# Masks by recurrences on VectorE and a new order of the first stretch in a chain of attention, feed-forward and routed experts

## The chip, the cores and the metric

The kernel runs on one core of a Trainium2 chip. The metric is the device time of one execution in microseconds. Instructions of each engine (TensorE, VectorE, ScalarE, GpSimd) run in the order in which they were issued to that engine; loads and stores are issued by the sequencers of SyncE (SP) or ScalarE and move on 16 DMA engines. The profile calls TensorE's matmuls PE and its weight loads PEld, VectorE DVE, ScalarE ACT and GpSimd POOL.

## The reference

Three layers stand one behind the other, on 1536 tokens of width 512 (2 batches, 8 heads of 64, sequence 768).

1. Linear attention with decay. Each head has a decay `lam`. Per block of 64 positions the output is `(q k^T * Dmask) v + (q * lam^(pos+1)) state`, with `Dmask[i, j] = lam^(i-j)` for `i >= j` and 0 elsewhere, and then `state = lam^64 * state + (k * lam^(63-pos))^T v`.
2. A dense feed-forward: `h = x w_in` (2048 wide), `g = elu(h)`, `x = g w_out`. The two weight matrices come in as 64-bit floats.
3. A routed layer: `logits = x w_gate` (8 experts), a skip score `x w_skip`; a token whose score is positive goes to its best expert, `x + gate * relu(x w1[e]) w2[e]`; the others pass through.

Everything is wanted at float32 accuracy.

## The kernel before, in words

The attention is rewritten over chunks of 128 tokens, 12 in all, 6 to a batch. Three chunks make a block of 384 tokens, and there are four blocks. For a chunk `c` the plan knows these steps, which also name what is issued: `S` scores on PE (16 matmuls, L251), `M` the multiplication of the scores by the decay mask on DVE (two halves, L261), `KD` and `QD` the products of k and q with powers of the decay on POOL (L284, L278), `KV` k times v on PE (L454), `ST` and `DEC` the update of the state (ST on DVE, L481, for chunk 0 on ACT; DEC on ACT, L461), `V` and `I` the two products that make the output on PE (L293), and `XH` and `XL` the split of the output into a high part (ACT, L437) and a remainder (DVE, L441), which together are the activations `xT` of the feed-forward.

The feed-forward works with pairs of high part and remainder too, and three matmuls stand for one product. A weight piece `f` (16 of them, 1 MB each as 64-bit words) is turned into such a pair by `CV` (ACT, L162), three bit operations `B0`, `B1`, `B2` (DVE, L174, L177, L180), `HI` (ACT, L185) and `LO` (DVE, L191). One step `n` of the feed-forward is `F1` (12 matmuls of 384 columns, L506), the activation `R`, `X` (ACT, L511, L514), `E` (DVE, L526), `GH` (ACT, L532), `GL` (DVE, L537), and `F2` (9 matmuls of 512 columns, L553). There are 64 steps, 16 for each of four blocks; the first 32 take the first two blocks in a mixed order, so that a weight piece is wanted only about every second step.

The string `PLAN` (L38) lists the order in which the steps of the first batch's attention and of feed-forward steps 0 to 22 are issued; each engine sees its own steps in that order. The rest is issued by loops. Late in the kernel the last block is routed: transposes (L593), logits (L608: 128 weight columns against 9 moving columns, for four parts, two instructions each), a pick of the expert on DVE (L666 to L676), one-hot tiles (L699), and matmuls that gather the rows of expert 0 (L1055, L1024); then eight experts follow, each with matmuls L1112 and L1137.

Before the plan begins the tables of the decay are made. `lam` is loaded to 8 partitions of `z8`; seven multiplications (L774) double a row of powers up to `lam^128`; the row is written to DRAM (`z_dr`, L777) and read back by one DMA as `mask`, 128 partitions of 8 overlapping windows (L788). Two kinds of matmuls spread the powers: a transpose for `kd` (L823) and four matmuls for `lp` (L825), which hold the factors of KD and QD. Groups of matmuls on zeros (`warm`, L817) stand ahead and behind: 6 and 5 of them, two instructions each.

The loads: `lam` goes out on SP, `f0`, `v0` and `q0` on ACT's queue. The next SP issues are ordered one after another by hand: the write of `z_dr`, q1, v1, the read of `mask`, and then q2, v2, q3, v3, f1, q4, v4, f2, q5, v5, f3, f4 and the rest (here `q` is the pair of q and k for the scores, `v` the pair of k and v by rows, 0.5 MB each).

Of the kernel before, what the change touches and what calls it, by code (L numbers as in the profile page):

```python
# [61 lines left out]
def kernel(  # L62
# [203 lines left out]

    qd_t = {}

    def at_qd(c):
        if c % CPS:  # L270
            if c == 1:
                qd = mid.tile([P, 2, TB], F32, tag="g", name="g", bufs=3)
                qd = qd.rearrange("p s t -> p (s t)")[:, 0:4 * P].rearrange("p (k i) -> p k i", k=4)
            elif c < CPS:
                qd = ph[0].tile([P, 4, P], F32, tag="qd", name="qd", bufs=1)
            else:
                qd = t2()
# [471 lines left out]


    if True:
        alloc_chunk(0)
        alloc_chunk(1)
        alloc_chunk(2)
        z8 = ph[0].tile([H, ZW], F32, tag="v", name="z8", bufs=2)
        sel = t2()[0:H]
        nc.sync.dma_start(out=z8[:, P + 1:P + 2], in_=lam.rearrange("(h o) -> h o", o=1))
        load_ff(0, nc.scalar)
        dma_kv(0, nc.scalar)
        dma_kq(0, nc.scalar)  # L760
        nc.vector.memset(z8[:, 0:P], 0.0)
        nc.vector.memset(z8[:, P:P + 1], 1.0)
# [15 lines left out]
        zt = z_dr[:, :]
        toep = bass.AP(tensor=zt.tensor, offset=zt.offset + 1, ap=[[1, P], [ZW, H], [1, P]])
        for c in range(CPB, CPS):  # L780
            alloc_chunk(c)
        lead = zw.ins
        with tc.issue_after(lead):
            lead = dma_kq(1).ins
        with tc.issue_after(lead):
            lead = dma_kv(1).ins
        with tc.issue_after(lead):
            mr = nc.sync.dma_start(out=mask, in_=toep)  # L788
# [34 lines left out]
        nc.tensor.transpose(out=kdb[:, 0:H], in_=z8[:, P:2 * P], identity=ident[0:H, 0:H])  # L823
        for k in range(4):
            nc.tensor.matmul(out=lpb[:, k * P:(k + 1) * P], lhsT=sel[:, k, :],  # L825
                             rhs=z8[:, P + 1:2 * P + 1], start=True, stop=True)
        warm(idle_bank, WARM[1])
        nc.vector.tensor_copy(out=kd, in_=kdb[:, 0:H].rearrange("p (h o) -> p h o", o=1))
        nc.scalar.activation(out=lp, in_=lpb.rearrange("p (k i) -> p k i", k=4), func=ACTF.Copy)
# [502 lines left out]
```

## Time and profile before

| | us |
|---|---|
| median of three executions | 442.74 (440.9 to 442.75) |
| the profiled execution: its time | 444.0 |
| its span in the trace | 441.8 |

| engine | busy in the span |
|---|---|
| PE | 426.9 us, 97% |
| PEld | 374.1 us, 85% |
| DVE | 326.3 us, 74% |
| ACT | 239.5 us, 54% |
| POOL | 74.1 us, 17% |

Times in the profile count from the start of the span; the 2.2 us by which the execution is longer lie around it. The ends of matmuls are modelled, so a busy PE may still be held up: the count of matmuls in a stretch tells more than its busy time. [...] DVE's busy share is an average over very unlike stretches: it is nearly full from 25 to 100 us, where weight pieces are converted, and about 60% from 100 to 200 us.

### The profile page before, as it was taken

How to read it: one execution, taken by the hardware profiler on the slowest of the kernel's cores; microseconds unless marked ns; L12 is line 12 of the kernel's file. 1: busy time of each engine (PE TensorE's matmuls, PEld its weight loads, DVE VectorE, ACT ScalarE, POOL GpSimd, SP SyncE). 2: the span in 40 equal slices, each digit the busy share in tenths (PEclk: the TensorE clock that was granted, in tenths of full speed). 3: DMA queues.
4: the chain of work that ended last, by engine and by line, in shares of the span. 5: the costliest groups of instructions: out<-in, count | busy, mean ns of one | idle time of the engine just before them, and what ended most of it. 6: DMA issues, size and time to landing. Idle time of an engine off the chain costs nothing.

```text
span 441.8 us, 8027 instructions
## 1 busy us (share of the span) xinstructions
PE 426.9 (97%) x3087; PEld 374.1 (85%) x3087; DVE 326.3 (74%) x701; ACT 239.5 (54%) x401; POOL 74.1 (17%) x104
## 2 busy tenths in 40 slices
...
GB/s 310 394 420 415 274 47 82 244 121 191 32 2 72 6 116 99 144 24 191 56 134 62 73 190 191 119 118 174 162 208 194 304 326 372 376 370 384 159 2 35
DMA packets 28704, 79.45 MB, mean 180 GB/s; under 512 B 4306, under 2 KB 9434, under 8 KB 26608
## 3 DMA queue, kind: packets, MB, share of 16 engines
...
## 4 chain that ended last, share of the span: by engine, by line
PE 68%; DVE 15%; DMA 6%; issue 5%; ACT 3%; SPq 2%; POOL 1%; POOLq 0%; ACTq 0%; DVEq 0%
PE h L506 23%; PE y L553 18%; PE h L1112 8%; PE y L1137 6%; PE aux L553 5%; DVE v L177 3%; DMA big<-in_wff_dram 2%; DMA xe<-blank 2%; DVE v L180 2%; DVE wa L191 2%; DVE g L537 1%; ACT v L162 1%; PE aux L1123 1%; DVE v L174 1%; DMA z_dr<-z 1%
## 5 line engine op out<-in xcount | busy, mean ns | idle before, releaser
L506 PE MATMUL h<-xT,wa 128*128 128x384 f32 x480 | 90.6, 338 | 0.1
L506 PEld LDWEIGHTS h<-xT,wa 128*128 128x128 f32 x480 | 84.1, 188 | 3.2 <-ACT xT L437 0.3
L553 PE MATMUL y<-wa,g 128*128 128x512 f32 x270 | 68.5, 396 | 0.3 <-DVE g L537 0.3
L532 ACT ACTIVATE g<-e 128x384 fp32r<-128x384 f32 x64 | 33.4, 522 | 48.3 <-DVE e L526 48.3
L553 PEld LDWEIGHTS y<-wa,g 128*128 128x128 f32 x270 | 49.6, 188 | 9.7 <-DVE g L537 0.7
L511 ACT ACTIVATE e<-h 128x384 f32<-128x384 f32 x64 | 31.0, 485 | 48.7 <-PE h L506 48.5
L506 PE MATMUL h<-xT,wb 128*128 128x384 f32 x288 | 54.6, 338 | 0.0
L526 DVE SCALAR_TENSOR_TENSOR e<-e,h 128x384 f32<-128x384 f32 x64 | 35.2, 550 | 26.2 <-ACT e L514 26.2
L506 PEld LDWEIGHTS h<-xT,wb 128*128 128x128 f32 x288 | 50.8, 188 | 2.4 <-issue 0.5
L537 DVE TENSOR_TENSOR g<-e,g 128x384 fp32r<-128x384 f32 x64 | 36.0, 563 | 9.0 <-ACT g L532 8.9
L553 PE MATMUL y<-wb,g 128*128 128x512 f32 x162 | 40.6, 395 | 0.0
L635 DVE CUSTOM_DVE_ANT_0 zrow<-x,big 128x512 int8<-128x512 f32 x54 | 38.2, 707 | 0.6
L1112 PE MATMUL h<-wa,xgT 128*128 128x512 f32 x144 | 36.0, 397 | 0.1
L514 ACT ACTIVATE e<-e 128x384 f32<-128x384 f32 x64 | 33.6, 525 | 2.0
L553 PEld LDWEIGHTS y<-wb,g 128*128 128x128 f32 x162 | 29.8, 188 | 5.6
L140 DVE TENSOR_TENSOR wa<-big,wa 128x1024 fp32r<-128x1024 f32 x22 | 26.6, 1234 | 6.5 <-ACT wa L139 6.3
L1112 PEld LDWEIGHTS h<-wa,xgT 128*128 128x128 f32 x144 | 26.4, 188 | 5.7 <-ACT xgT L584 0.3
...
L352 POOL TENSOR_TENSOR big<-big,mask 128x512 f32<-128x512 f32 x6 | 7.4, 1230 | 114.4 <-DMA big<-in_kv_dram 114.4
L139 ACT ACTIVATE wa<-big 128x1024 fp32r<-128x1024 f32 x22 | 22.4, 1057 | 3.1 <-DMA big<-in_wex_dram 3.1
L140 DVE TENSOR_TENSOR wa<-ahead,wa 128x1024 fp32r<-128x1024 f32 x18 | 21.7, 1249 | 2.9 <-ACT wa L139 2.7
L1137 PE MATMUL y<-wa,ht 128*128 128x512 f32 x96 | 23.7, 398 | 0.0
...
## 6 DMA issues: line engine op xcount, KB each, us to landing
...
```

The costliest lines, as they stand in the source:

```text
L139: nc.scalar.activation(out=w[:, 0, cs], in_=src, func=ACTF.Copy)
L140: nc.vector.tensor_tensor(out=w[:, 1, cs], in0=src, in1=w[:, 0, cs].bitcast(F32), op=ALU.subtract)
L506: nc.tensor.matmul(out=h, lhsT=w[:, wi, k * P:(k + 1) * P], rhs=xT[b][:, xi, k, :], start=(j == 0), stop=(j == 11))
L511: nc.scalar.activation(out=e, in_=h_t[n], func=ACTF.Relu, scale=-1.0)
L514: nc.scalar.activation(out=e_t[n], in_=e_t[n], func=ACTF.Exp, scale=-1.0)
L526: nc.vector.scalar_tensor_tensor(out=e, in0=e, scalar=-1.0, in1=h_t.pop(n), op0=ALU.add, op1=ALU.max)
L532: nc.scalar.activation(out=g[:, 0, :], in_=e, func=ACTF.Copy)
L537: nc.vector.tensor_tensor(out=g[:, 1, :], in0=e_t.pop(n), in1=g[:, 0, :].bitcast(F32), op=ALU.subtract)
L553: nc.tensor.matmul(out=y_t[b, t], lhsT=g[:, gi, t * P:(t + 1) * P], rhs=w[:, wi, 512:1024], start=(f == 0 and i == 0), stop=(f == NF - 1 a ...
L635: nc.vector.tensor_tensor_reduce(out=junk, in0=x2_t[c][:, 0:DM], in1=cols[0][:, slot * DM:(slot + 1) * DM], scale=1.0, scalar=0.0, op0=ALU ...
L1112: nc.tensor.matmul(out=h, lhsT=xgT_t[e][:, xi, k * P:(k + 1) * P], rhs=w_t[NF + 8 * e + k][:, wi, j * 512:(j + 1) * 512], start=(i == 0), ...
L1137: nc.tensor.matmul(out=y, lhsT=ht[:, hi, k, :], rhs=w_t[NF + 8 * e + 4 + k // 2][:, wi, (k % 2) * 512:(k % 2) * 512 + 512], start=(i == 0) ...
```

## The change

- `mask` is no longer read from DRAM. A tile `anti` (1 on the anti-diagonal, 0 elsewhere) is made by GpSimd; `lam` is spread to all partitions by one matmul (a row of ones against a diagonal of `lam`) and copied to `lam_b`; and eight scans on DVE (`MR:h`, one for each head) run `x[i] = lam * x[i-1] + anti[i]` along 128 elements. They are steps of the plan.
- The row of powers comes from one scan on 8 partitions; `lp` is spread by four matmuls as before, and its copy on ACT is a step of the plan (`LC`). `kd` is now the last column of `mask`.
- All loads go out on SP, in the order of the string `LOADS`; the DRAM tile `z_dr` and the write and read of it are gone.
- Zero matmuls: groups of 4, 1 and 5 in place of 6 and 5.
- `QD` writes in place over q for chunks 1 to 5; that of chunk 5 is on DVE (`QE:5`). The remainders of weight pieces 1 and 2 are made on POOL (`LP:1`, `LP:2`).
- The plan has a new order throughout; its first lines stand below.
- The logits of the routing are computed six times side by side (54 columns in place of 9); only the first nine are used.

```diff
+COPIES = 6
-ZW = 264
+LOADS = "f0 q0 q1 v0 v1 q2 v2 q3 v3 f1 v4 q4 f2 q5 v5 f3 f4 f5 f6 f7 f8 f9"
 PLAN = """
-CV:0 B0:0 KD:0 B1:0 KV:0 S:0 ST:0 B2:0 QD:1 HI:0 KD:1 I:1 LO:0 S:1 DEC:1 KV:1 M:0,0 M:0,1
-ST:1 V:0 QD:2 M:1,0 S:2 XH:0 KD:2 M:1,1 XL:0 I:2 M:2,0 S:3 M:2,1 DEC:2 QD:3 KV:2 M:3,0
-KD:3 V:1 ST:2 V:2 M:3,1 XH:1 CV:1 XL:1 I:3 XH:2 B0:1 V:3 DEC:3 QD:4 XL:2 B1:1 F1:0 XH:3
-KD:4 B2:1 S:4 R:0 XL:3 X:0 HI:1 M:4,0 KV:3 M:4,1 CV:2 ST:3 S:5 E:0 V:4 M:5,0 GH:0 GL:0 I:4
-M:5,1 LO:1 KV:4 DEC:4 QD:5 F2:0 B0:2 XH:4 ST:4 CV:3 XL:4 I:5 B1:2 V:5 B2:2 F1:1 XH:5 HI:2
-XL:5 B0:3 LO:2 F1:2 R:1 X:1 CV:4 E:1 B1:3 F1:3 GH:1 R:2 GL:1 X:2 B2:3 F2:1 R:3 E:2 B0:4
...
+MR:5 MR:2 MR:0 MR:6 CV:0 S:0 MR:1 B0:0 MR:4 MR:7 B1:0 MR:3 KD:0 B2:0 KD:1 M:0,0 M:0,1 S:1 LC:0
+KV:0 QD:1 ST:0 M:1,1 KD:2 HI:0 M:1,0 V:0 LO:0 XH:0 S:2 I:1 KV:1 M:2,1 QD:2 V:1 DEC:1 S:3 XH:1
+ST:1 M:2,0 I:2 DEC:2 KV:2 QD:3 M:3,0 CV:1 KD:3 XL:0 V:2 M:3,1 V:3 ST:2 I:3 XL:1 KD:4 XH:2 XL:2
+F1:0 B0:1 XH:3 B1:1 XL:3 B2:1 DEC:3 S:4 CV:2 M:4,1 KV:3 M:4,0 ST:3 R:0 HI:1 QD:4 X:0 E:0 S:5 V:4
+I:4 M:5,0 M:5,1 LP:1 KV:4 GH:0 DEC:4 CV:3 GL:0 V:5 B0:2 QE:5 B1:2 F2:0 XH:4 ST:4 B2:2 I:5 XH:5
+B0:3 XL:5 HI:2 F1:1 XL:4 F1:2 LP:2 R:1 X:1 E:1 GH:1 R:2 B1:3 X:2 GL:1 CV:4 B2:3 F1:3 F2:1 E:2
...
-    kd = nx[:, 0:H].rearrange("p (h o) -> p h o", o=1)
+    kd = mask[:, :, P - 1:P]
...
-    def conv_lo(f):
-        eng = nc.gpsimd if f in ON_POOL else nc.vector
+    def conv_lo(f, eng=None):
+        eng = eng or nc.vector
...
-            nc.gpsimd.tensor_tensor(out=qd, in0=kq_t[c][:, 1], in1=lp, op=ALU.mult)
+            qd = kq_t[c][:, 1] if c < CPS else t2()
+            (eng or nc.gpsimd).tensor_tensor(out=qd, in0=kq_t[c][:, 1], in1=lp, op=ALU.mult)
...
-            nc.tensor.matmul(out=lg[:, 0:E + 1], lhsT=x2T[:, k, :], rhs=wg[:, k, :],
+            nc.tensor.matmul(out=lg[:, 0:COPIES * (E + 1)].rearrange("p (o e) -> p o e", o=COPIES),
+                             lhsT=x2T[:, k, :],
+                             rhs=wg[:, k:k + 1, :].to_broadcast([P, COPIES, E + 1]),
...
+        nc.sync.dma_start(out=lam8, in_=lam.rearrange("(h o) -> h o", o=1))
+        loads = LOADS.split()
+        for item in loads[:3]:
+            load(item)
...
+        nc.gpsimd.affine_select(out=anti, in_=anti, pattern=[[1, P]], compare_op=ALU.not_equal,
+                                fill=1.0, base=1 - P, channel_multiplier=1)
...
-            nc.vector.tensor_scalar(out=z8[:, P + 1 + n:P + 1 + 2 * n], in0=z8[:, P + 1:P + 1 + n],
-                                    scalar1=z8[:, P + n:P + n + 1], scalar2=None, op0=ALU.mult)
-        zw = nc.sync.dma_start(out=z_dr[:, 0:2 * P + 1], in_=z8[:, 0:2 * P + 1])
+        nc.vector.tensor_scalar(out=diag8, in0=ident[0:H, 0:H], scalar1=lam8, scalar2=None, op0=ALU.mult)
+        nc.vector.tensor_tensor_scan(out=powers[0:H], data0=lam8.to_broadcast([H, P]),
+                                     data1=zrow[0:H], initial=1.0, op0=ALU.mult, op1=ALU.add)
+        for item in loads[3:]:
+            load(item)
...
-        WARM = (6, 5)
+        WARM = (4, 1, 5)
...
+        nc.tensor.matmul(out=lamb[:, 0:H], lhsT=ones8, rhs=diag8, start=True, stop=True)
+        warm(idle_bank, WARM[1])
...
+        nc.vector.tensor_copy(out=lam_b, in_=lamb[:, 0:H])
+
+        def mask_row(h):
+            nc.vector.tensor_tensor_scan(out=mask[:, h, :], data0=lam_b[:, h:h + 1].to_broadcast([P, P]),
+                                         data1=anti, initial=0.0, op0=ALU.mult, op1=ALU.add)
```

## Rows read from the trace of the kernel before

**Rows 1.** Busy time by stretch, all engines; (x) counts instructions; PEclk, DMA share, GB/s last.
```profile
5.00:10.00 5.00, 3.69 (x38) 3.27 (x37) 2.72 (x3) 2.21 (x4) 1.43 (x2) 0.75 1.02 414
10.00:15.00 5.00, 5.00 (x50) 4.33 (x50) 3.88 (x4) 2.39 (x6) 3.02 (x2) 0.56 0.99 337
...
20.00:25.00 5.00, 4.89 (x85) 4.46 (x80) 4.14 (x8) 3.29 (x7) 2.51 (x3) 1.00 1.02 415
...
40.00:50.00 10.00, 10.00 (x56) 9.35 (x55) 9.63 (x16) 7.46 (x13) 0.00 (x0) 1.00 0.99 400
```
**Rows 2.** The same view, F1's matmuls (L506) alone: PE, PEld, then clock and DMA.
```profile
38.80:98.10 59.30, 33.12 (x180) 31.40 (x180) 1.00 0.64 178
```
**Rows 3.** The same stretch, F2's matmuls (L553) alone.
```profile
38.80:98.10 59.30, 28.91 (x120) 22.20 (x120) 1.00 0.64 178
```
**Rows 4.** Chain of waits, early and steady part: start, us, what.
```profile
4.27 4.17 DMA z_dr<-z
11.24 10.97 DMA big<-in_wff_dram
...
106.28 2.08 PE y L553 x9
108.36 2.09 PE h L506 x12
```
**Rows 5.** Timeline of the first 41 us: start, us, engine, line, operation [idle before].
```profile
6.06 1.12 ACT L162 ACTIVATE v<-big 128x1024 f32<-128x1024 f32 x1
7.21 1.43 DVE L174 TENSOR_SCALAR v<-v 128x1024 int32<-128x1024 int32 x1 [2.47 <-ACT v L162]
...
14.38 1.28 DVE L261 TENSOR_TENSOR pm_store<-h,mask 128x512 f32<-128x512 f32 x2
...
24.12 0.68 DVE L441 TENSOR_TENSOR xT<-aux,xT 128x512 fp32r<-128x512 f32 x1
24.72 1.72 DVE L177 SCALAR_TENSOR_TENSOR v<-big,v 128x1024 int32<-128x1024 int32 x1
...
25.31 2.03 POOL L284 TENSOR_TENSOR wa<-wa,nx 128x512 f32<-128x512 f32 x1
...
26.47 1.95 DVE L180 SCALAR_TENSOR_TENSOR v<-big,v 128x1024 int32<-128x1024 int32 x1
...
36.29 0.86 DVE L481 TENSOR_TENSOR state<-aux,state 64x256 f32<-64x256 f32 x2
...
38.89 6.66 PE L506 MATMUL h<-xT,wa 128*128 128x384 f32 x36
...
40.86 0.68 DVE L174 TENSOR_SCALAR v<-v 128x1024 int32<-128x1024 int32 x1
```
**Rows 6.** Groups by form, DVE and POOL: line, tiles, count, busy us, mean ns.
```profile
L763 DVE MEMSET zrow<- 128x128 f32 x1 | 0.2, 165 | 0.0
...
L177 DVE SCALAR_TENSOR_TENSOR v<-wb,v 128x1024 int32<-128x1024 int32 x1 | 1.2, 1215 | 0.0
...
L284 POOL TENSOR_TENSOR wb<-wb,nx 128x512 f32<-128x512 f32 x3 | 4.1, 1371 | 5.1 <-DMA wb<-in_kv_dram 5.1
```
**Rows 7.** Chain of waits in the routing of the last block.
```profile
323.01 0.87 PE aux L593 x8
...
328.29 1.70 PE aux L1055 x8
...
330.05 1.90 PE aux L1024 x8
```
**Rows 8.** Stretches as in rows 1, in the routing of the last block.
```profile
328.00:330.00 2.00, 2.00 (x15) 1.94 (x14) 1.32 (x8) 0.00 (x0) 0.00 (x0) 0.59 1.03 422
330.00:332.00 2.00, 2.00 (x15) 1.94 (x14) 0.36 (x1) 0.00 (x0) 0.00 (x0) 0.55 1.02 422
```
**Rows 9.** Timeline of the same part: logits, and a DVE instruction on 128x128.
```profile
327.24 1.05 PE L608 MATMUL aux<-wg,t 128*128 128x9 f32 x8
...
328.24 0.35 DVE L699 SCALAR_TENSOR_TENSOR e<-places,y,pick 128x128 f32<-128x128 f32 x1
```

More of the change, by code (lines that the diff above doesn't have):

```diff
@@ new lines @@
+F1:0 B0:1 XH:3 B1:1 XL:3 B2:1 DEC:3 S:4 CV:2 M:4,1 KV:3 M:4,0 ST:3 R:0 HI:1 QD:4 X:0 E:0 S:5 V:4
+I:4 M:5,0 M:5,1 LP:1 KV:4 GH:0 DEC:4 CV:3 GL:0 V:5 B0:2 QE:5 B1:2 F2:0 XH:4 ST:4 B2:2 I:5 XH:5
+B0:3 XL:5 HI:2 F1:1 XL:4 F1:2 LP:2 R:1 X:1 E:1 GH:1 R:2 B1:3 X:2 GL:1 CV:4 B2:3 F1:3 F2:1 E:2
+B0:4 F1:4 HI:3 GH:2 B1:4 GL:2 R:3 LO:3 X:3 R:4 E:3 X:4 F2:2 B2:4 GH:3 E:4 GL:3 F1:5 CV:5 F2:3
+B0:5 HI:4 GH:4 LO:4 CV:6 B1:5 GL:4 B0:6 R:5 B2:5 F1:6 X:5 HI:5 R:6 E:5 B1:6 F2:4 X:6 GH:5 LO:5
+F1:7 CV:7 E:6 GL:5 F1:8 GH:6 B2:6 R:7 B0:7 F2:5 X:7 E:7 B1:7 HI:6 GH:7 GL:7 GL:6 LO:6 R:8 X:8
@@ new lines @@
+CV:8 F2:6 E:8 GH:8 B2:7 B0:8 F1:9 B1:8 HI:7 GL:8 F1:10 F2:7 LO:7 B2:8 R:9 X:9 E:9 CV:9 B0:9 R:10
+X:10 E:10 HI:8 F2:8 B1:9 GH:9 LO:8 B2:9 CV:10 B0:10 GL:9 B1:10 GH:10 HI:9 GL:10 F1:11 F1:12 R:11
+LO:9 X:11 R:12 CV:11 E:11 X:12 F2:9 B2:10 B0:11 E:12 GH:11 F1:13 HI:10 GL:11 R:13 B1:11 B2:11
+F2:10 GH:12 F2:11 GL:12 LO:10 F2:12 HI:11 CV:12 LO:11 CV:13 X:13 B0:12 B1:12 E:13 B0:13 F1:14
+B2:12 F1:15 GH:13 R:14 X:14 E:14 GL:13 B1:13 GH:14 GL:14 F2:13 R:15 HI:12 LO:12 B2:13 X:15 CV:14
+E:15 GH:15 B0:14 F1:16 GL:15 F2:14 B1:14 F2:15 R:16 X:16 E:16 HI:13 GH:16 F1:17 LO:13 CV:15
@@ L58 @@
+B2:14 GL:16 R:17 X:17 B0:15 HI:14 B1:15 F1:18 F2:16 E:17 GH:17 R:18 B2:15 X:18 GL:17 LO:14 F1:19
+R:19 E:18 F2:17 F1:20 HI:15 GH:18 GL:18 X:19 E:19 F2:18 GH:19 R:20 F1:21 X:20 E:20 GH:20 LO:15
+GL:19 F2:19 R:21 X:21 E:21 GL:20 F1:22 R:22 F2:20 GH:21 X:22 GL:21
 """
@@ L88 @@
     wide = wff.dtype == mybir.dt.int64
-    z_dr = dram.tile([H, ZW], F32, name="z_dr")
     xe = dram.tile([E * NTOK, XW], F32, name="xe")
@@ L267, with at_qd, at_kdec @@
     qd_t = {}
-    def at_qd(c):
+    def at_qd(c, eng=None):
         if c % CPS:
[L271 to L277, printed above, removed]
-            nc.gpsimd.tensor_tensor(out=qd, in0=kq_t[c][:, 1], in1=lp, op=ALU.mult)
+            qd = kq_t[c][:, 1] if c < CPS else t2()
+            (eng or nc.gpsimd).tensor_tensor(out=qd, in0=kq_t[c][:, 1], in1=lp, op=ALU.mult)
             qd_t[c] = qd
-    def at_kdec(c):
+    def at_kdec(c, eng=None):
         if c % CPS != CPS - 1:
             k3 = kv_t[c][:, 0, :].rearrange("p (h d) -> p h d", h=H)
-            nc.gpsimd.tensor_tensor(
+            (eng or nc.gpsimd).tensor_tensor(
                 out=k3, in0=k3, in1=kd.to_broadcast([P, H, D]), op=ALU.mult
@@ L751 @@
     if True:
[L752 to L762, printed above, removed]
-        nc.vector.memset(zrow, 0.0)
+        tab = ph[0].tile([P, 3 * P + 2 * H + 1], F32, tag="v", name="tab", bufs=2)
@@ new lines, with load @@
+        anti, lam_b = tab[:, 0:P], tab[:, P:P + H]
+        ones8, diag8 = tab[0:H, P + H:2 * P + H], tab[0:H, 2 * P + H:2 * P + 2 * H]
+        powers, lam8 = tab[:, 2 * P + 2 * H:3 * P + 2 * H], tab[0:H, 3 * P + 2 * H:]
+        sel = t2()
+        nc.sync.dma_start(out=lam8, in_=lam.rearrange("(h o) -> h o", o=1))
+        for c in range(CPS):
+            alloc_chunk(c)
+        def load(item):
+            kind, eng, n = item[0], nc.scalar if item[1] == "a" else nc.sync, int(item.lstrip("qvfa"))
+            {"q": dma_kq, "v": dma_kv, "f": load_ff}[kind](n, eng)
@@ L764 @@
+        loads = LOADS.split()
+        for item in loads[:3]:
+            load(item)
+        nc.vector.memset(zrow, 0.0)
+        nc.vector.memset(ones8, 1.0)
+        nc.vector.memset(powers, 0.0)
+        make_identity(nc, ident)
+        nc.gpsimd.memset(anti, 0.0)
+        nc.gpsimd.affine_select(out=anti, in_=anti, pattern=[[1, P]], compare_op=ALU.not_equal,
+                                fill=1.0, base=1 - P, channel_multiplier=1)
         nc.gpsimd.memset(sel, 0.0)
-        nc.gpsimd.affine_select(out=sel.rearrange("h k (j i) -> h k j i", j=2),
-                                in_=sel.rearrange("h k (j i) -> h k j i", j=2),
+        nc.gpsimd.affine_select(out=sel[0:H].rearrange("h k (j i) -> h k j i", j=2),
+                                in_=sel[0:H].rearrange("h k (j i) -> h k j i", j=2),
@@ L777 @@
-        zw = nc.sync.dma_start(out=z_dr[:, 0:2 * P + 1], in_=z8[:, 0:2 * P + 1])
[L778 to L788, printed above, removed]
```

49 lines of the change are left out of this document (8 added, 41 removed).

## The prediction

> **What bounds the kernel now.** I read four views: busy time by stretch, the chain of waits, the timeline of the first 41 us, and the groups by form. First the steady part, to learn what an earlier start is worth. In the chain of waits F1 and F2 alternate without a gap, 2.09 us for 12 matmuls and 2.08 us for 9 [rows 4]. From 38.80 to 98.10 us the trace has 180 matmuls of F1 and 120 of F2 [rows 2, 3]. At the steady rate these are 180 x 2.09/12 = 31.4 us and 120 x 2.08/9 = 27.7 us, together 59.1 of 59.3 us. So TensorE is full from the start of `F1:1` at 38.89 us [rows 5] onwards, although DVE is at 9.63 of 10 us in the same part [rows 1] and stands on the chain too. What brings `F1:1` forward goes straight to the end, if DVE comes forward by as much.
>
> Second, what sets 38.89 us. Before it DVE is the engine with the long queue. It gets its first conversion at 7.21 us, after the copy of `f0` on ACT [rows 5]. From there its idle time is small: 1.12 us from 10 to 15 and 0.86 us from 20 to 25 us [rows 1]. The first mask multiplication, `M:0`, begins only at 14.38 us [rows 5]; the chain has the 4.17 us of the DMA that writes `z_dr`, behind which the mask's read was queued, and 10.97 us for `f1`, issued behind it at 11.24 us [rows 4]. Third, TensorE: its granted clock averages 0.75 from 5 to 10 and 0.56 from 10 to 15 us [rows 1], near its lower level, and it does so again at 328 to 332 us, 0.59 and 0.55 [rows 8].
>
> **The change, part by part. Tables.** The seven doublings, two memsets and the copy of `kd` go from DVE, and a few small instructions and the scan of powers come; both lie before `f0` is there, where DVE idles (2.47 us before 7.21 [rows 5]). I cost them at nothing: without that cover their order of magnitude is a handful of instructions between 0.165 us [rows 6] and 0.35 us [rows 9], about 1 us. The eight mask rows are new. No scan is in the trace; from below a 128x128 memset takes 0.165 us [rows 6], from above I take a 128x512 two-input instruction, 0.68 us (`XL`) [rows 5]. My value is 0.35 us, the 128x128 instruction with a per-partition scalar [rows 9]. Five rows stand before `B0:0`; they fit between lam's spreading, which I put at 3.8 us, and 6.6 us. Three stand behind: 3 x 0.35 = 1.05 us on DVE's queue (0.5 to 2.0; at 0.68 the first five overrun as well, 3.8 + 3.4 = 7.2, by 0.6).
> [...]
>
> **Loads.** `f0` goes first on one queue instead of sharing with `v0` and `q0`, so it should land some 0.6 us earlier: `B0:0` at 6.6 us. `f1` now has `f0` and four chunks ahead of it, with itself 6.3 MB; at 0.415 MB/us [rows 1] that is 15.2 us after a first byte at about 2.2, 17.4 us. It landed at 11.24 + 10.97 = 22.2 us. DVE reaches `B0:1` at about 22 us, so both idle times of 1.12 and 0.86 us go. What was moved back is `v0`: some 8.9 us. `KD:0` waits for it and for the eighth mask row; on POOL `KD:1`, `QD:1` and the others queue behind, and on PE `KV:0` and `V:0`, for which the masked scores are not ready before 12 us anyway.
>
> **DVE up to XL:2.** From 6.6 us: `B` of `f0` 0.68 + 2 x 1.22, three mask rows 1.05, eight halves of `M` at 0.64, `LO:0` 1.22, `ST:1` and `ST:2` at 0.86, three `XL` at 0.68 [rows 5, 6]: 3.1 + 1.05 + 5.1 + 1.2 + 1.7 + 2.0 = 14.2. To it comes what POOL's instructions cost DVE. `B0:0` took 1.43 instead of 0.68 us, and later `B1` and `B2` took 1.72 and 1.95 instead of 1.22 us beside a `KD` of 2.03 us [rows 5, 6]. I take 0.9 us: the end of `XL:2` is 21.7 us against 24.8, a lead of 3.1.
>
> **DVE from there to ST:4.** Before: 24.80 to 37.15 [rows 5], 12.35 us. Out: `LO:1`, 1.22. In: `B0:1` 0.68, `QE:5` 0.68, `B1:2` 1.22, all of which stood outside this stretch. `LP:1` on POOL is 128x1024 where a 128x512 product has a mean of 1.37 us [rows 6], so about 2.7 us (1.4 to 4.1, twice the 2.03 of rows 5), and costs DVE some 0.8 us more by contention (0 to 3.3). 12.35 - 1.22 + 2.58 + 0.8 = 14.5, so `ST:4` ends at 36.2 instead of 37.15. Then only `I:5` stands before `F1:1` on PE, not `I:5` and `V:5`: about 0.9 us, `F1:1` at 37.1, 1.8 us earlier.
>
> **The next step.** `B2:2` ends at 37.4, `HI:2` at 38.5, and `LP:2` behind it on POOL at 41.2 (39.9 to 42.6). `F1:3` wants this remainder at 37.1 + 2 x 2.1 + 0.35 = 41.65. With the long end PE waits 0.9 us; I take 0.2. The front is worth **-1.6 us** (+2.4 to -3.5). From then DVE is ahead: it does not have `LO:2` (1.22 us).
>
> **Zero matmuls.** One fewer, before any data is there: nothing. That they keep the clock up until the first scores I do not count on: between 7 and 12 us only `S:0`, `S:1` and `KV:0` can run. The cover is that DVE, not PE, sets `V:0` and the rest; without it each stretch at the lower level doubles PE's work in it, at most 1.7 us more.
>
> **Wider logits.** Eight instructions of 9 columns took 1.05 us [rows 9], and eight of 128 columns 0.87 [rows 7], so 54 columns should cost nothing (up to 24 x 0.04 = 0.9 us, if the columns were added bare). What they may give: after the logits the clock falls to 0.59 and 0.55 [rows 8], and the two groups of eight take 1.70 and 1.90 us instead of the 0.87 of the same size [rows 7]; 0.83 + 1.03 = 1.86 us is lost there. DVE's picks would then end last before the second gather, so I take **-1.4 us** (0 to -1.8). The expert part behind it follows, as PE's chain is unbroken there.
>
> **Sum.** -1.6 - 1.4 = -3.0. Against the profiled execution, 444.0 = 441.8 + 2.2: 441.0. That execution is 1.3 us above the median of 442.74, so by the median 439.7.
>
> **Rivals.** *POOL holds DVE.* The two `LP` take 4.1 us each and DVE waits for all of it, so that the 1.22 saved costs up to 4.1. For it: `B1` and `B2` lost 0.50 + 0.73 us beside one `KD` that itself took 2.03 us [rows 5, 6]. Against it: much of DVE's work there (M, XL, ST) reads the scores and sums, and `M:0` kept 0.64 us. `ST:4` is then 39.5, `F1:1` 40.4, `LP:2` ends at 45.9 where `F1:3` wants it at 44.9: +1.5 + 1.0 = +2.5; with the clock falling in the routing as before 445.2, slower. It decides from about 3 us a piece. [...]
> *Only one half comes.* Either the wider logits don't hold the clock (54 columns are still fewer than 128): -1.6, 441.1; or mask rows, contention and a late `KD:0` eat the lead and only the routing gains: -1.4, 441.3. No change that could be measured.
> *The front gives more.* Rows of 0.17 us (-0.5), no contention (-1.4 or more) and no wait for `LP:2`: -3.5 in front, with the routing 437.8.
>
> **How the numbers follow.** Forecast 0.45; more in front 0.17; one half 0.26; POOL holds DVE 0.12. About 0.5% (2.2 us) is what a measurement of this kernel can tell from no change, so faster is below 440.5 and slower above 445.0. Four fifths of the forecast's chance, all of the larger gain and a fifth of the one half are faster: 0.36 + 0.17 + 0.05 = 0.58. Slower is most of the POOL case, 0.10; the rest 0.32. The range reaches to 436.8, a microsecond beyond the larger gain, and to 443.7, the POOL case with the routing's gain.
>
> **What would show it.** `f1` landing near 17.4 us; `B0:0` at 6.6; mask rows of 0.35 us; `M:0` before 12 us; the end of `XL:2` near 21.7, `ST:4` near 36.2, `F1:1` near 37.1; 180 and 120 matmuls in the 59 us behind it; a clock of 1.00 through the routing and two gathers of 0.87 us. It is wrong if DVE's steps beside `LP:1` are stretched by more than 2 us, if a row takes over 0.6 us, if PE has gaps between `F1:1` and the end of the plan, or if the experts don't follow the routing.

## The result, and the profile after

The changed kernel takes 437.3 us (median of four executions, 436.81 to 437.99) against 442.58 us for the kernel before (four, 440.9 to 442.75): a ratio of 0.989 with a 95% interval of 0.9861 to 0.9919. It is faster by 5.3 us; 3.0 were forecast. The profiled execution took 436.92 us, its span is 434.8.

Where the time went is best seen by cutting both spans at three events that both kernels have. Starts are from the timeline and the chain of waits; each kernel was profiled a second time in an experiment below.

| stretch, us | before | before again | after | after again |
|---|---|---|---|---|
| to the start of `F1:1` | 38.89 | 38.86 | 35.14 | 35.09 |
| from there to the chain's 21 matmuls of F2 before the last routing | 279.30 | 278.48 | 277.70 | 278.81 |
| from there to the first expert matmul | 15.81 | 14.21 | 14.24 | 14.24 |
| from there to the end of the span | 107.80 | 107.75 | 107.72 | 107.66 |
| span | 441.8 | 439.3 | 434.8 | 435.8 |

Only the first line differs by more between the kernels than between two executions of one kernel: 3.75 and 3.77 us. So the front carries the gain. The routing's 1.57 us in the first pair is gone in the second.

The timeline of the front of the changed kernel (start, duration, engine, line, operation, idle time before). The lines are L161 for CV, L173, L176 and L179 for B0, B1 and B2, L184 for HI, L188 for LO and LP, L258 for M, L269 for QD, L275 for KD, L432 for XL, L472 for ST, L497 for F1, L528 for GL, L810 for a mask row:

```profile
4.28 1.69 DVE L810 TENSOR_TENSOR_SCAN mask<-tab 128x128 f32<-128x128 f32 x5
...
7.30 0.69 DVE L173 TENSOR_SCALAR v<-v 128x1024 int32<-128x1024 int32 x1 [1.33 <-ACT v L161]
...
11.12 1.28 DVE L258 TENSOR_TENSOR pm_store<-h,mask 128x512 f32<-128x512 f32 x2
...
14.87 1.60 DVE L188 TENSOR_TENSOR wa<-v,wa 128x1024 fp32r<-128x1024 f32 x1 [1.27 <-ACT wa L184]
...
21.54 1.06 POOL L275 TENSOR_TENSOR wa<-wa,mask 128x512 f32<-128x512 f32 x1 [0.84 <-DMA wa<-in_kv_dram]
21.97 0.69 DVE L432 TENSOR_TENSOR xT<-aux,xT 128x512 fp32r<-128x512 f32 x1
...
23.30 1.23 DVE L176 SCALAR_TENSOR_TENSOR v<-big,v 128x1024 int32<-128x1024 int32 x1
...
25.04 1.22 DVE L179 SCALAR_TENSOR_TENSOR v<-big,v 128x1024 int32<-128x1024 int32 x1
...
28.00 2.37 POOL L188 TENSOR_TENSOR wa<-v,wa 128x1024 fp32r<-128x1024 f32 x1 [0.60 <-ACT wa L184]
...
28.84 0.68 DVE L258 TENSOR_TENSOR pm<-aux,mask 128x512 f32<-128x512 f32 x1
...
30.13 0.66 DVE L528 TENSOR_TENSOR g<-e,g 128x384 fp32r<-128x384 f32 x1
...
33.15 0.87 DVE L472 TENSOR_TENSOR state<-aux,state 64x256 f32<-64x256 f32 x2
...
35.14 6.51 PE L497 MATMUL h<-xT,wa 128*128 128x384 f32 x36
...
36.89 2.40 POOL L188 TENSOR_TENSOR wa<-v,wa 128x1024 fp32r<-128x1024 f32 x1 [5.11 <-ACT wa L184]
```

Read it from the end. The 36 matmuls of `F1:1` to `F1:3` run through from 35.14 us. `LP:2`, which `F1:3` needs, ends on POOL at 39.29, and no stall follows. `ST:4` ends at 34.02, where it ended at 37.15 [rows 5]. Between the end of `XL:2` (22.66) and that lie 11.36 us, against 12.35 before. In that stretch `B1:1` and `B2:1` take 1.23 and 1.22 us, not 1.72 and 1.95 [rows 5]: `KD:4` (21.54 to 22.60) is over before `B1:1` begins. Beside `LP:1` (28.00 to 30.37) run steps that read the scores or sums from PSUM, `M` at 0.68, and one short step on SBUF, `GL`, at 0.66 (0.55 in the second profile).

The busy time by stretch (PE, PEld, DVE, ACT, POOL, then the clock granted to TensorE as a share of the full one, DMA share, GB/s), to set beside [rows 1]:

```profile
0.00:5.00 5.00, 3.70 (x15) 3.38 (x16) 2.36 (x9) 1.49 (x2) 2.65 (x11) 1.00 0.56 172
5.00:10.00 5.00, 5.00 (x33) 4.78 (x34) 3.67 (x9) 1.61 (x2) 0.00 (x0) 1.00 1.01 415
10.00:15.00 5.00, 3.97 (x74) 3.49 (x72) 3.73 (x7) 1.96 (x4) 4.83 (x4) 1.00 1.02 410
15.00:20.00 5.00, 5.00 (x104) 4.71 (x102) 4.94 (x8) 3.36 (x10) 4.20 (x4) 1.00 1.02 411
```

From 15 to 20 us DVE is full, and the 16 DMA engines are full from 5 us on (a share of 1.01 and 1.02). From 10 to 15 us DVE still idles 1.27 us: `LO:0` (14.87 above) waits that long for `HI:0` on ACT. The chain of waits of the changed kernel (start, us, what), behind the front and in the routing:

```profile
35.21 6.44 PE h L497 x36
...
312.84 4.83 PE y L544 x21
...
319.94 0.83 PE h L599 x8
...
323.02 0.95 PE aux L1040 x8
324.03 1.00 PE aux L1009 x8
...
327.08 5.79 PE h L1097 x24
```

The logits of 54 columns take 0.83 us for eight, the two gathers 0.95 and 1.00 us, not the 1.70 and 1.90 of [rows 7].

### The profile page after: what moved, and what is told of

It reads as the page before. It is cut to its first block, busy times and chain, and to the rows that moved or that the text cites. A ratio compares the mean times of both kernels' runs of the same rounds, so it can differ in the third digit from the quotient of the medians.

```text
span 434.8 us, 8034 instructions
## 1 busy us (share of the span) xinstructions
PE 422.6 (97%) x3086; PEld 371.1 (85%) x3086; DVE 322.1 (74%) x703; ACT 239.0 (55%) x401; POOL 77.8 (18%) x107
## 4 chain that ended last, share of the span: by engine, by line
PE 82%; DVE 6%; issue 4%; DMA 3%; ACT 2%; POOL 1%; SPq 0%; POOLq 0%; ACTq 0%
PE h L497 29%; PE y L544 21%; PE h L1097 8%; PE aux L544 8%; PE y L1122 6%; PE aux L284 2%; DMA big<-in_wex_dram 1%; PE y L284 1%; DVE wa L139 1%; DMA big<-in_wff_dram 1%; PE aux L1108 1%; PE aux L599 1%; DMA out_dram<-o,ix 1%; PE aux L584 1%; PE aux L1077 1%
## 5 line engine op out<-in xcount | busy, mean ns | idle before, releaser
L497 PE MATMUL h<-xT,wa 128*128 128x384 f32 x480 | 89.8, 337 | 0.0
L497 PEld LDWEIGHTS h<-xT,wa 128*128 128x128 f32 x480 | 83.6, 188 | 3.0 <-issue 0.6
L497 PE MATMUL h<-xT,wb 128*128 128x384 f32 x288 | 54.2, 336 | 0.0
L517 DVE SCALAR_TENSOR_TENSOR e<-e,h 128x384 f32<-128x384 f32 x64 | 35.1, 549 | 24.2 <-ACT e L505 23.9
L497 PEld LDWEIGHTS h<-xT,wb 128*128 128x128 f32 x288 | 50.5, 188 | 2.5 <-issue 0.5
L528 DVE TENSOR_TENSOR g<-e,g 128x384 fp32r<-128x384 f32 x64 | 36.2, 566 | 12.7 <-ACT g L523 12.7
L139 DVE TENSOR_TENSOR wa<-ahead,wa 128x1024 fp32r<-128x1024 f32 x18 | 21.7, 1250 | 2.7 <-ACT wa L138 2.5
```

The costliest lines, as they stand in the source:

```text
L139: nc.vector.tensor_tensor(out=w[:, 1, cs], in0=src, in1=w[:, 0, cs].bitcast(F32), op=ALU.subtract)
L497: nc.tensor.matmul(out=h, lhsT=w[:, wi, k * P:(k + 1) * P], rhs=xT[b][:, xi, k, :], start=(j == 0), stop=(j == 11))
L517: nc.vector.scalar_tensor_tensor(out=e, in0=e, scalar=-1.0, in1=h_t.pop(n), op0=ALU.add, op1=ALU.max)
L528: nc.vector.tensor_tensor(out=g[:, 1, :], in0=e_t.pop(n), in1=g[:, 0, :].bitcast(F32), op=ALU.subtract)
```

## The experiments

There are twelve runs, the first two of unchanged kernels. The fifth leaves out the matmuls on zeros, and the sixth adds work that nothing reads. Each time is compared with executions of the kernel before on the same chip.

**The kernel before, again, and the changed kernel, again** (`x1_before_again`, `x2_after_again`, no edit): which differences belong to the kernels, and which to one execution?

> The kernel before, unchanged, for a second profile. Between the start of F1:1 and the last F2 group the profiled execution before took 279.3 us (38.89 to 318.19) and the one after 277.7 us (35.14 to 312.84), though the instructions are the same. Theory A: that 1.6 us belongs to the one profiled execution of before (444.0, against a median of 442.7); then F1 and F2 take 2.08 and 2.06 us here too and the stretch about 277.7. Rival B: the change speeds that stretch up; then it is again about 279.3 here.

> The changed kernel, unchanged, as the level on this chip for the other runs of this call. 437.3 us, ratio 0.988 to 0.989; F1:1 at 35.1 us in its profile.

The kernel before took 441.51 us in this one execution (22 others on the same chip: median 442.99, 440.56 to 446.32), with this chain of waits in the routing and these stretches (columns as above):

```profile
317.34 4.82 PE y L553 x21
...
327.45 0.99 PE aux L1055 x8
328.50 1.00 PE aux L1024 x8
```
```profile
10.00:15.00 5.00, 4.18 (x64) 3.62 (x64) 3.84 (x4) 2.98 (x7) 3.33 (x3) 1.00 1.00 345
328.00:330.00 2.00, 2.00 (x24) 1.98 (x24) 1.21 (x7) 0.00 (x0) 0.00 (x0) 1.00 1.03 424
```

The same program that showed 0.56 from 10 to 15 us and 0.59 from 328 to 330 [rows 1, 8] now shows 1.00 in both places, and gathers of 0.99 and 1.00 us. In slices of 0.5 us the first profile reads 0.50, the lower level of the prediction, from 8.0 to 14.0 us and from 328.5 to 331.5, and 1.00 around them; one slice on either side of each is at 0.53 to 0.88. The low clock in the routing belonged to one execution. In front it cost nothing: `F1:1` starts at 38.86 with the full clock and at 38.89 without. The changed kernel took 438.49 (437.52 to 439.99), ratio 0.9894 [0.9851, 0.9937]. The two second profiles (441.51 and 437.95 us) differ by 3.56 us; the front alone makes 3.77.

**Logits of 9 columns again** (`x3_logits_9`).

```diff
-COPIES = 6
+COPIES = 1
```

> The changed kernel with the logits 9 columns wide again. Theory A (the wider logits hold the granted clock up through the gathers of the last block): the clock falls to 0.5 at the gathers as before, the two groups of eight take 1.70 and 1.90 us again, and it is 1.6 us slower than the changed kernel, 438.9. Rival B (the clock there depends on where the run stands in time, not on the columns): no fall, 437.3.

438.32 us (11 executions), ratio 0.9897 [0.9866, 0.9928]: the same as with 54 columns. Its chain of waits in the routing:

```profile
322.20 0.79 PE h L599 x8
...
323.94 0.99 PE aux L1040 x8
324.99 1.00 PE aux L1009 x8
```

In this execution the clock holds with 9 columns as well, as the gathers of 0.99 and 1.00 us show. The wider logits gain nothing that can be measured and cost 0.04 us for eight matmuls.

**The two remainders back on DVE** (`x4_lo_on_dve`).

```diff
-I:4 M:5,0 M:5,1 LP:1 KV:4 GH:0 DEC:4 CV:3 GL:0 V:5 B0:2 QE:5 B1:2 F2:0 XH:4 ST:4 B2:2 I:5 XH:5
-B0:3 XL:5 HI:2 F1:1 XL:4 F1:2 LP:2 R:1 X:1 E:1 GH:1 R:2 B1:3 X:2 GL:1 CV:4 B2:3 F1:3 F2:1 E:2
+I:4 M:5,0 M:5,1 LO:1 KV:4 GH:0 DEC:4 CV:3 GL:0 V:5 B0:2 QE:5 B1:2 F2:0 XH:4 ST:4 B2:2 I:5 XH:5
+B0:3 XL:5 HI:2 F1:1 XL:4 F1:2 LO:2 R:1 X:1 E:1 GH:1 R:2 B1:3 X:2 GL:1 CV:4 B2:3 F1:3 F2:1 E:2
```

> The changed kernel with the remainders of weight pieces 1 and 2 on DVE, as before. Theory A (POOL makes them at 2.4 us each beside DVE instructions that it hardly holds up, so 2 x 1.22 us of DVE's queue are won, and DVE sets the start of F1:1): F1:1 is 1.2 us later, and the time 1.2 us longer, 438.5. Rival B (PE sets it, or DVE gives the time back): under 0.4 us, 437.5.

440.72 us, ratio 0.9943 [0.9917, 0.997], some 2 us slower than the changed kernel. The timeline shows `LO:1` on DVE and `F1:1` late by as much:

```profile
30.34 1.22 DVE L188 TENSOR_TENSOR wa<-v,wa 128x1024 fp32r<-128x1024 f32 x1
...
36.43 3.78 PE L497 MATMUL h<-xT,wa 128*128 128x384 f32 x19
```

36.43 - 35.14 = 1.29 us for an instruction of 1.22. So where `LP:1` stands, POOL's 2.37 us take almost nothing from DVE. Another 0.27 us comes behind it: in the chain of waits the 36 matmuls of `F1:1` to `F1:3` take 6.71 us with `LO:2` on DVE, against 6.44.

**No matmuls on zeros** (`x5_no_zeros`).

```diff
-        WARM = (4, 1, 5)
+        WARM = (0, 0, 0)
```

> The changed kernel without any of the matmuls on zeros. Theory A (DVE, not TensorE, sets the start of F1:1; the second profile of before reached F1:1 at 38.93 us at the upper clock throughout, the first at 38.89 with the clock at its lower level from 7.8 to 14.6 us): even if the clock is lower in the first 15 us, F1:1 is within 0.5 us of 35.2 and the time within 0.6 us of the changed kernel. Rival B (the zeros carry a part of the gain): the granted clock is low through the first chunks, PE reaches F1:0 2 us late and the time is 1.5 us longer or more.

439.28 us where the kernel before took 443.86: ratio 0.9891 [0.9872, 0.9911], no difference. The 16 matmuls of the first scores take 2.08 us (1.79 with the zeros, in the profile of the changed kernel above, and 1.16 for those of `S:2` in both; the clock column reads 1.00 in both). Nobody waits for that: the first mask multiplication begins at 11.08 us (11.12 with the zeros) and `F1:1` at 35.27.

```profile
11.08 1.28 DVE L258 TENSOR_TENSOR pm_store<-h,mask 128x512 f32<-128x512 f32 x2
```

**POOL kept busy beside B1:1 and B2:1** (`x6_pool_beside`): two sums of 128x512 are added on POOL.

```diff
-ST:1 M:2,0 I:2 DEC:2 KV:2 QD:3 M:3,0 CV:1 KD:3 XL:0 V:2 M:3,1 V:3 ST:2 I:3 XL:1 KD:4 XH:2 XL:2
+ST:1 M:2,0 I:2 DEC:2 KV:2 QD:3 M:3,0 CV:1 KD:3 XL:0 V:2 M:3,1 V:3 ST:2 I:3 XL:1 KD:4 XH:2 XL:2 PX:0 PX:0
...
+        def extra(i):
+            j = ph[0].tile([P, 4, P], F32, tag="qd", name="qd", bufs=1)
+            x = xT[0][:, :, :, 2 * P:3 * P].bitcast(F32)
+            nc.gpsimd.tensor_tensor(out=j, in0=x[:, 1], in1=x[:, 0], op=ALU.add)
```

> The changed kernel with two more 128x512 two-input instructions on POOL (they write a tile that nothing reads), which start when XL:2 has ended, beside B0:1, B1:1 and B2:1 on DVE. Theory A (what the first stretch gained is above all that POOL no longer runs beside DVE's steps that read SBUF alone; there it costs each 0.5 to 0.7 us, as in 1.72 and 1.95 against 1.22 us before): B1:1 or B2:1 take 1.7 to 1.95 us again, F1:1 is 1.0 to 1.4 us later, the time too. Rival B (contention is not on the path): under 0.4 us.

440.93 us, ratio 0.9935 [0.9911, 0.996], about 1.9 us slower than the changed kernel. The timeline beside the added work (L867):

```profile
23.36 0.69 DVE L432 TENSOR_TENSOR xT<-aux,xT 128x512 fp32r<-128x512 f32 x1
...
24.13 3.94 POOL L867 TENSOR_TENSOR qd<-xT 128x512 f32<-128x512 f32 x2 [0.87 <-DVE xT L432]
...
24.69 2.23 DVE L176 SCALAR_TENSOR_TENSOR v<-big,v 128x1024 int32<-128x1024 int32 x1
...
26.84 0.68 DVE L432 TENSOR_TENSOR xT<-aux,xT 128x512 fp32r<-128x512 f32 x1
...
27.44 1.72 DVE L179 SCALAR_TENSOR_TENSOR v<-big,v 128x1024 int32<-128x1024 int32 x1
...
28.04 2.25 POOL L269 TENSOR_TENSOR wa<-wa,lp 128x512 f32<-128x512 f32 x1
...
35.95 0.86 DVE L472 TENSOR_TENSOR state<-aux,state 64x256 f32<-64x256 f32 x2
```

`B1:1` and `B2:1`, with two inputs in SBUF, are 1.00 and 0.50 us longer; `XL`, between them, which reads PSUM, keeps its 0.68. From the end of `XL:2` to that of `ST:4` it is 36.81 - 24.05 = 12.76 us, 1.40 more than in the changed kernel. This is about the 0.50 + 0.73 = 1.23 us that the two instructions lost in the kernel before, and which the prediction kept. (`F1:1` is 2.9 us late in this profile; the other half, a late `XL:2`, comes with a granted clock of 0.72 from 10 to 15 us.)

**The old order with the new tables and loads** (`x7_old_plan`): behind the eight mask rows and the copy of `lp` stands the plan of before, word for word, with its own tiles for `qd`.

```diff
+MR:5 MR:2 MR:0 MR:6 MR:1 MR:4 MR:7 MR:3 LC:0
+CV:0 B0:0 KD:0 B1:0 KV:0 S:0 ST:0 B2:0 QD:1 HI:0 KD:1 I:1 LO:0 S:1 DEC:1 KV:1 M:0,0 M:0,1
...
```

> The changed kernel (tables by scans, new loads, zeros, wider logits) with the order of before: all eight mask rows first, then the old plan, with LO:1, LO:2 on DVE, QD:5 on POOL and q's products in tiles of their own. Theory A (the order, with what it puts on POOL, makes most of the 3.8 us in front): F1:1 at 37.5 us or later, 2.4 us or more behind the changed kernel. Rival B (tables and loads make it): F1:1 at 36 us or before.

445.44 us (12 executions), ratio 1.0037 [1.0018, 1.0056]: not faster but slightly slower than the kernel before. The timeline (lines lie 2 to 8 further down in this kernel; 36.48 and 36.68 are `B0:2` and `QD:5`):

```profile
10.17 1.46 POOL L283 TENSOR_TENSOR wb<-wb,mask 128x512 f32<-128x512 f32 x1 [6.86 <-DMA wb<-in_kv_dram]
...
14.46 1.74 DVE L190 TENSOR_TENSOR wa<-v,wa 128x1024 fp32r<-128x1024 f32 x1 [3.75 <-ACT wa L186]
...
16.12 1.27 DVE L260 TENSOR_TENSOR pm_store<-h,mask 128x512 f32<-128x512 f32 x2
...
36.48 0.69 DVE L175 TENSOR_SCALAR v<-v 128x1024 int32<-128x1024 int32 x1
...
36.68 1.65 POOL L277 TENSOR_TENSOR qd<-wa,lp 128x512 f32<-128x512 f32 x1 [7.77 <-issue]
...
41.06 2.21 PE L505 MATMUL h<-xT,wa 128*128 128x384 f32 x11
```

With `v0` fourth in the loads, `KD:0` waits until 10.17; ACT's first state copy and `HI:0` follow, DVE waits 3.75 us for `HI:0` with the mask multiplications queued behind it. `XL:2` ends at 26.35, 1.55 us later than before, and `F1:1` starts at 41.06, 2.17 later. The rest is not the order alone: the granted clock is 0.76 from 30 to 35 us in this profile, and `M:5,1` waits 0.46 us for a product there. The mean clock of eleven of the twelve executions is 0.984 to 0.987, where the ten executions of the changed kernel have 0.990 to 0.997. With the old order the loads and tables give nothing; the gain needs the new order of the first two blocks.

**Loads nearer to the old order** (`x8_loads_near_old`).

```diff
-LOADS = "f0 q0 q1 v0 v1 q2 v2 q3 v3 f1 v4 q4 f2 q5 v5 f3 f4 f5 f6 f7 f8 f9"
+LOADS = "f0 v0 q0 q1 v1 q2 v2 q3 v3 f1 q4 v4 f2 q5 v5 f3 f4 f5 f6 f7 f8 f9"
```

> The changed kernel with v0 in front of q0 and q1, and q4 in front of v4, as before. Theory A (KD:0 waits for the eighth mask row at 10.1 us, so an earlier v0 gives nothing, and q0 some 1.2 us later delays S:0 from 8.5 to about 9): 0.0 to 0.5 us longer. Rival B (the new order of loads is what brings the front forward): 1 us or more.

440.51 us, ratio 0.9917 [0.9885, 0.9949], some 1.1 us slower than the changed kernel (the intervals overlap). The six executions lie apart: three at 439.1 to 439.9 us, three at 441.2 to 443.3. The profiled one, at 442.4 us, belongs to the second group. Its timeline shows why the place of `v4` ahead of `q4` can count:

```profile
23.03 1.37 POOL L275 TENSOR_TENSOR wa<-wa,mask 128x512 f32<-128x512 f32 x1 [2.26 <-DMA wa<-in_kv_dram]
...
23.51 1.97 DVE L176 SCALAR_TENSOR_TENSOR v<-big,v 128x1024 int32<-128x1024 int32 x1
...
25.93 1.28 POOL L269 TENSOR_TENSOR wa<-wa,lp 128x512 f32<-128x512 f32 x1 [1.53 <-PE aux L248]
...
26.00 2.29 DVE L179 SCALAR_TENSOR_TENSOR v<-big,v 128x1024 int32<-128x1024 int32 x1
...
38.79 3.41 PE L497 MATMUL h<-xT,wa 128*128 128x384 f32 x18
```

`KD:4` waits for `v4` 1.5 us longer, falls beside `B1:1`, pushes it back, and `B2:1` then falls beside `QD:4`: 0.74 + 1.07 = 1.8 us. `F1:1` is 3.65 us late here; behind the two instructions the granted clock is 0.66 from 30 to 35 us, and two products take 1.97 and 1.82 us in place of 1.09 and 1.04. Whether the first group escapes the overlap was not seen. The other half of this edit, `v0` ahead of `q0` and `q1`, was not run by itself.

**A further gain in front?** Four kernels, each on top of the one before it, attack the idle time that DVE has left from 10 to 15 us. First all mask rows ahead of `B0:0`, and `HI:0` ahead of `KV:0` (`x9_rows_early`):

```diff
-MR:5 MR:2 MR:0 MR:6 CV:0 S:0 MR:1 B0:0 MR:4 MR:7 B1:0 MR:3 KD:0 B2:0 KD:1 M:0,0 M:0,1 S:1 LC:0
-KV:0 QD:1 ST:0 M:1,1 KD:2 HI:0 M:1,0 V:0 LO:0 XH:0 S:2 I:1 KV:1 M:2,1 QD:2 V:1 DEC:1 S:3 XH:1
+MR:5 MR:2 MR:0 MR:6 MR:1 MR:4 MR:7 MR:3 CV:0 S:0 B0:0 B1:0 KD:0 B2:0 KD:1 M:0,0 M:0,1 S:1 LC:0 HI:0
+KV:0 QD:1 ST:0 M:1,1 KD:2 M:1,0 V:0 LO:0 XH:0 S:2 I:1 KV:1 M:2,1 QD:2 V:1 DEC:1 S:3 XH:1
```

> The changed kernel with all eight mask rows ahead of B0:0 (DVE idles 1.33 us there, three rows take 1.1) and with HI:0 on ACT ahead of ST:0 (LO:0 waited 1.27 us for it). Theory A (DVE's queue sets the front): M:0 begins at 10.4 instead of 11.1 us, LO:0 at 13 instead of 14.9, F1:1 1 to 2 us earlier, time 1 to 2 us shorter. Rival B (the chain v0, KD:0 on POOL, KV:0, ST:0, I:1 sets it; v0 lands at 10.15 us as the profile with the old plan shows): LO:0 comes earlier, but DVE then waits for the scores of chunk 2 and for KV:1, ST:1 stays at 17.0 and F1:1 within 0.4 us of 35.2.

Then `v0` ahead of `q1` (`x10_v0_second`):

```diff
-LOADS = "f0 q0 q1 v0 v1 q2 v2 q3 v3 f1 v4 q4 f2 q5 v5 f3 f4 f5 f6 f7 f8 f9"
+LOADS = "f0 q0 v0 q1 v1 q2 v2 q3 v3 f1 v4 q4 f2 q5 v5 f3 f4 f5 f6 f7 f8 f9"
```

> The same with v0 ahead of q1 in the loads. Theory A (DVE's queue): no more than the run before it. Rival B (the chain from v0): v0 lands at 8.9 us, KD:0 starts at 8.9 instead of 10.2, ST:1 at 15.8 to 16.2, F1:1 at 34.0 to 34.5, and the time is 0.7 to 1.2 us shorter than the changed kernel's.

Then `f0` on ACT's queue, by the letter `a` (`x11_f0_act`):

```diff
-LOADS = "f0 q0 v0 q1 v1 q2 v2 q3 v3 f1 v4 q4 f2 q5 v5 f3 f4 f5 f6 f7 f8 f9"
+LOADS = "fa0 q0 v0 q1 v1 q2 v2 q3 v3 f1 v4 q4 f2 q5 v5 f3 f4 f5 f6 f7 f8 f9"
```

> The same as the run before it with the load of f0 issued on ACT's queue, 0.47 us earlier (0.81 instead of 1.28 us, as in the kernel before). If f0's landing sets the front: B0:0 at 6.9 and F1:1 0.4 us earlier; if f0 now shares the engines with q0 it lands no earlier than 6.1 and nothing changes or q0 is later.

Last `f1` ahead of `q3` and `v3` (`x12_f1_early`):

```diff
-LOADS = "fa0 q0 v0 q1 v1 q2 v2 q3 v3 f1 v4 q4 f2 q5 v5 f3 f4 f5 f6 f7 f8 f9"
+LOADS = "fa0 q0 v0 q1 v1 q2 v2 f1 q3 v3 v4 q4 f2 q5 v5 f3 f4 f5 f6 f7 f8 f9"
```

> The run before it (rows and HI:0 early, v0 second, f0 on ACT's queue) with f1 loaded ahead of q3 and v3. In the three runs before it DVE came 0.4 to 0.8 us ahead by 20.5 us and then waited, since CV:1 on ACT waited for f1 (landed at 20.0 to 20.4 us) and XH:2 stood behind it. Theory A (f1's landing sets the front now): CV:1 starts before 18.5 us, XL:2 at 21.2 instead of 21.65, F1:1 at 34.2 to 34.5 instead of 34.8, the time about 0.5 us shorter than the run before. Rival B (q3, 2.5 us later, holds S:3 up by as much as f1 gains): F1:1 at 34.8 or later.

| kernel | us | ratio | 95% | `M:0` | `F1:1` |
|---|---|---|---|---|---|
| rows early | 438.01 | 0.9886 | 0.9859 to 0.9913 | 10.46 | 35.29 |
| and `v0` second | 438.93 | 0.99 | 0.9872 to 0.9928 | 11.14 | 35.22 |
| and `f0` on ACT | 438.04 | 0.9883 | 0.9854 to 0.9912 | 10.83 | 34.81 |
| and `f1` early | 438.87 | 0.993 | 0.9904 to 0.9956 | 10.83 | 35.25 |

None is measurably faster than the changed kernel. With `v0` second, `F1:1` was expected at 34.0 to 34.5 us: `KD:0` does start early, at 8.75 us, but now runs beside `B2:0`, which takes 1.97 us in place of 1.20, and `M:0` is back at 11.14. The timeline of the first shows where the 0.66 us gained at `M:0` are given back:

```profile
20.42 1.19 ACT L161 ACTIVATE v<-big 128x1024 f32<-128x1024 f32 x1 [0.84 <-DMA big<-in_wff_dram]
...
22.12 0.69 DVE L432 TENSOR_TENSOR xT<-aux,xT 128x512 fp32r<-128x512 f32 x1 [0.91 <-ACT xT L428]
```

ACT waits for `f1`, and the copy that `XL:2` needs is queued behind. With `f1` early, the wait moves: `S:3` then begins at 17.36, held 0.87 us by the landing of `q3`.

The DMA engines are full from 5 us on (a share of 0.99 to 1.05 up to 40 us with `f1` early), and in these four profiles what DVE gains early ends in a wait for a load. This speaks for the loads as the bound of the front now; it is argued, as no run loads less. With `f0` on ACT's queue the first step is 0.34 us earlier (`B0:0` at 6.96), and `F1:1` 0.33 earlier, too little to be told in the time.

## Why the prediction was right in its direction and too small

**TensorE is full behind `F1:1`: right.** The front's gain arrives at the end of the span. In the 59.3 us from 35.1 the trace of the changed kernel has 185 matmuls of F1 and 117 of F2, 302 in all, where before there were 300. The middle stretch of the four profiles agrees within 1.6 us, with no order between the kernels in the clean pair (278.48 and 278.81).

**Tables: right.** Five rows in one go take 1.69 us, 0.34 each, where 0.35 was taken; `M:0` begins at 11.12, before 12. The eight records have a mean of 0.41 us. Moving the last three rows ahead of `B0:0` (`x9_rows_early`) did not bring `F1:1` forward.

**Loads: wrong in two sizes.** `f0` was to land 0.6 us earlier, because it no longer shares a queue with `v0` and `q0`. It takes 4.84 us from issue to landing, and in the trace of before 4.8: sharing had cost nothing. But it is now issued behind `lam` on SP, at 1.28 instead of 0.81 us, so `B0:0` starts at 7.30, 0.7 later than forecast and no earlier than before (7.21, [rows 5]). `f1` was to land at 17.4; this issue (KB, us to landing) was made at 7.41 and landed at 20.2:

```profile
big<-in_wff_dram SPq DMA_DIRECT2D x1, 1024.0 KB, 12.8
```

By the stretches above, 5 x 0.172 + 15.2 x 0.412 = 7.1 MB had moved by then, 0.8 more than the 6.3 of `f1` and all ahead of it; so about 1.9 of the 2.8 us went to transfers queued behind it, and the rest to the first 5 us, with 172 GB/s. The landing of `f1` held nobody up in this profile, though: ACT's work ahead of `CV:1` ended at 20.24.

**DVE up to `XL:2`: 1.0 us too optimistic.** Its end came at 22.66, not 21.7. The late `B0:0` is 0.7 of this. For the rest two terms nearly cancel: of 0.9 us for contention about 0.4 came, on `LO:0` (1.60 us, not 1.22), but the idle time from 10 to 15 us, which was to go, stayed at 1.27 us. There `LO:0` waits for `HI:0`, which stands on ACT behind the first state copy and so behind `KD:0` (10.17); with `HI:0` moved ahead of that copy (`x9_rows_early`) DVE is busy for all of these 5 us.

**DVE from there to `ST:4`: this step failed.** It was put at 14.5 us and took 11.36. The 12.35 us of before, from which it started, hold contention with POOL: 0.50 on `B1:1`, 0.73 on `B2:1`, and 1.32 on `B0:2`, which took 2.00 us beside POOL's `QD:5` where its other occurrence takes 0.68 [rows 5]. I kept these 2.55 us and added 0.8 for `LP:1`. I also named one `KD` as the neighbour of both: `B1:1` (24.72 to 26.44) started under the `QD` ahead of it, the first row below, and only `B2:1` under `KD:4`. In the new order `KD:4` is early, `QD:5` is on DVE (0.68) and `LP:1` stands beside steps that read PSUM; what is left is about 0.2 us. 12.35 - 2.55 - 1.22 + 2.58 + 0.2 = 11.36, the measured stretch. The term was 3.1 us too long. Three rows of the timeline of before:

```profile
23.65 1.70 POOL L278 TENSOR_TENSOR qd<-wa,lp 128x512 f32<-128x512 f32 x1 [2.49 <-DMA wa<-in_kq_dram]
...
33.50 2.12 POOL L278 TENSOR_TENSOR qd<-wa,lp 128x512 f32<-128x512 f32 x1 [6.16 <-PE aux L293]
...
34.37 2.00 DVE L174 TENSOR_SCALAR v<-v 128x1024 int32<-128x1024 int32 x1
```

With both errors, and 0.2 us more than the 0.9 taken for PE's work after `ST:4`, 37.1 + 1.0 - 3.1 + 0.2 = 35.2: the start of `F1:1`. The parts of the missing 3.1 us are not equally well shown. For `B1:1` and `B2:1` (1.23) an experiment brings it back: POOL beside them costs 1.5 us in the two instructions and 1.4 in the stretch, and in the profile with the other order of `v4` and `q4` they lose 1.8. For `B0:2` (1.32) there is a comparison: with the old order and `QD:5` on POOL again, but begun 0.2 us after `B0:2` instead of 0.9 before it, `B0:2` takes 0.69 us and the POOL product is the one that is longer (1.65 us; the shortest of these take 1.26). For `LP:1`, put at 0.8, `LO:1` back on DVE made `F1:1` 1.29 us late, its full duration, so `LP:1` had cost DVE almost nothing.

**`LP:2`: nothing, not 0.2.** It takes 2.40 us where 2.7 was taken, and begins at 36.89.

**Zeros: right.** Without them the time is the same (a ratio of 0.9891 to the kernel before, 0.9894 with them).

**Wider logits: wrong.** The -1.4 us were read from a clock that fell in one execution of the kernel before. A second one has no such fall, and 9 columns in the changed kernel give the same time. So it is partly luck that the forecast of -3.0 lies as near as it does: of its two terms the routing's -1.4 did not come, and the front, put at -1.6, gave 3.75 us.

**The rivals.** "POOL holds DVE" is refuted where `LP:1` and `LP:2` stand: back on DVE they cost 2 us. What it expects is real elsewhere (`B1:1` 2.23 us in `x6_pool_beside` and `B2:1` 2.29 in `x8_loads_near_old`, instead of 1.22). In the cases above steps with two SBUF inputs were lengthened, those with one input in PSUM were not (0.68 us), and `B0:2`, with a single input in SBUF, was lengthened as well, from 0.68 to 2.00 us. What makes POOL and DVE hold each other up was not shown. "The front gives more" came closest: -3.5 in front (its own terms, 0.5, 1.4 and 0.2 on top of 1.6, make -3.7), against -3.75. Its condition, no contention, very nearly came true; its rows of 0.17 us and its routing part did not come.

**What stays open.** The medians differ by 4.5 to 5.3 us, the two clean profiles by 3.56, and the front makes 3.75. The second profile of before lies 1.5 us under the median of the 22 other executions on its chip, that of the changed kernel 0.5 under its own. Executions in which the clock falls in the routing, worth 15.81 - 14.21 = 1.6 us each, explain little of the rest: among those with a mean clock of 0.994 or more on that chip the medians still differ by 4.2 us (442.27 of seven, 438.03 of four). What is left is within the noise of these counts and was not located. Whether the wider logits make such falls rarer was not settled: the lowest mean clock is 0.985 in eleven executions with 9 columns (441.52 us) and 0.990 in ten of the changed kernel.
